# A list of operations searched anew: 44 fewer idle products and two sums of squares on TensorE

## The chip, the cores and the metric

One core of a Trainium2 chip runs the kernel. The time is that of the whole program on the device, in microseconds (us); of several runs the median is given. The engines are TensorE (PE, with PEld for its weight loads), VectorE (DVE), ScalarE (ACT), GpSimd (POOL) and SyncE (SP), which here only issues DMAs.

## What is computed

Linear attention over 4 batches, 8 heads, 576 positions of 64 numbers, then two feed-forward layers on the 2304 tokens of width 512:

```python
q_s = softmax(q, over the 64 numbers);  k_s = softmax(k, over the 576 positions)
kv  = einsum('bhsd,bhse->bhde', k_s, v);  x = einsum('bhsd,bhde->bhse', q_s, kv)   # -> (2304, 512)
xn  = x / sqrt(mean(x * x) + 1e-6) * rms_g
x   = (silu(xn @ w_gate) * (xn @ w_val)) @ w_out        # layer A, 1536 wide
out = softplus(x @ w_in) @ w2_out                       # layer B, 2048 wide
```

The weights arrive as 64-bit floats and are turned into 32-bit ones on the chip. Every large product is done as three products of rounded halves (`mm3`: high by high, high by low, low by high), on PE lines L838, L839 and L840.

## The kernel before

The tokens are cut into 6 blocks of 384 (3 chunks of 128), two blocks to a pair. Everything is unrolled, and the order of all instructions on all engines is one written list, `ORDER`, of some 3500 short tokens. Each token calls one function of the table `ops` and issues that function's instructions; the order of the tokens is the order in each engine's queue, and the semaphores between engines follow from the data. There is no loop and no priority beside it: an engine whose next instruction waits, waits. A last letter V, A or P picks VectorE, ScalarE or GpSimd for the step. `HOMES` says, for each kind of buffer, which of its places is taken in turn, so it changes whenever the list does.

The stages, as the list names them:

- Queries: `LQ` load, `Q0` maximum over the 64 numbers (L708), `QS` shift (L712), `QE` exponent, `QR`/`QI` sum and inverse (L721, L725), `QM` product (L732), `T`/`TC` transpose on PE (L740) and copy.
- Keys, per batch: `LK`/`LX` load, `K0` maxima over positions on DVE (L634, L636), `K1` transpose on PE (L644), `KM` maximum on DVE (L650), `K2` spread on PE (L657), `KS` subtract on DVE (L665), `KE` exponent on ACT, `K3` product with v on PE (L684), `K4` division on DVE (L692 to L695).
- Attention's output, per block j: `X0` product on PE (L770), `SQ` squares on ACT (L775), `XG` scaling, `XS` adds the four squares' tiles into one (L788, three steps a block), `X1` sums it over the partitions by a product with a column of ones on PE (L795, three products a block), `XD`/`XP` mean and inverse root, `X2` spread on PE (L811), `X3` scaling on DVE (L815), `HH`/`HL` the rounded halves (L835).
- Layer A: for the first four of the 12 slices of 128 plain products (`G`, `V`, `O`, with `S`, `A`, `AH`, `AL`); the other eight by seven products in place of eight (`M`, `C`, `D`, `SI`, `U`, `BH`, `BL`, `OP`, `OM`, `OC`).
- Layer B, by seven products too: `H`, `HC`, `HD`, `SP` (softplus), `BH`, `BL`, then `Y` into the output's tile, `YE` copy (L1203), `YO` store (L1214, L1211).
- Weights: `F` load, `CA` absolute value (L450, ACT or DVE), `CL` clamp (L455), `CD` shift and merge of the two words on DVE (L461, L465, L469), `CC`/`CS` halves (L483, L487), `ST`/`TU` out and back, `PS` sums for the seven products, `WH`/`WL` halves (L546, L552). Layer B's halves are stored with `KO` (L557, buffer `kept`) and loaded back with `WB` (L1164) for each of three pairs of blocks.
- `B.i.n` issues n products of the identity with itself (L885) that nobody reads: idle products. The list of before has twelve such tokens with 114 products, all in the first 65 us.

A matmul of 32-bit numbers that is not done in halves (`B`, `K1`, `K2`, `T`, `X1`, `X2`) shows as two rows of the trace.

At the end of the list, the two last `Y` complete the output's tile (pair 0, block 0, chunk 2); each tile has one copy of 512 columns and one or two stores.

Of the kernel before, what the change touches and what calls it, by code (L numbers as in the profile page):

```python
# [8 lines left out]
F32 = mybir.dt.float32  # L9
# [19 lines left out]
QM.0.1.0.P KS.0.0 CL.10.V B.5.6 LW.0 T.1 B.2.14 F.0 CD.10.0 K0.0.2.2.3.V QM.0.1.1.V K0.0.2.2.4.V K1.0.2 B.1.2 Q0.0.2  # L29
QS.0.2.0.P KM.0.2 K2.0.2 MV Q0.1.0 CA.3.A KE.0.0 CL.3.V F.5 LV.0.0.4 KS.0.2 CA.0.A CD.10.1 CL.0.V QS.1.0.0.P T.0 CD.0.0  # L30
CA.6.A QS.1.0.1.P KE.0.2 CL.6.V CD.0.1 CD.3.0 B.4.11 CD.3.1 K3.0.0 LV.0.4.8 CD.6.0 TC.0.A CA.5.A QE.1.0.0 CD.0.2 LK.1.2.2
T.2 CD.6.1 TC.2.A CD.10.2 K4.0.0 CD.3.2 K0.1.2.2.1.V LX.1 K3.0.2 K4.0.2 TC.1.A X0.0.1 SQ.0.1 X0.0.0 X0.0.3 LK.1.0.2 LG
QE.0.2.0 CC.3.A X0.0.2 K0.1.2.2.2.V SQ.0.0 CL.5.V SQ.0.2 F.2 CD.6.2 K0.1.0.2.1.V K0.1.2.2.3.V XS.0.0.1.V CA.2.A SQ.0.3
LQ.1.1 F.1 K0.1.0.2.2.V K0.1.0.2.3.V CC.0.A K0.1.2.2.4.V B.6.9 K1.1.2 XS.0.2.3.P CL.2.V F.7 QE.1.0.1 K0.1.0.2.4.V K1.1.0
XG.0.0.A KM.1.2 XS.0.0.2.P Q0.1.1 LW.1 CC.10.A XG.0.2.A QR.1.0 LV.1.4.8 QR.0.2.0 K2.1.2 QS.1.1.1.P CC.6.A QI.1.0 QS.1.1.0.P
B.7.4 KS.1.2 LK.2.2.2 CA.1.A X1.0 QI.0.2.0 KM.1.0 LV.1.0.4 XD.0 CS.10.V B.8.13 K2.1.0 QM.1.0.0.P KE.1.2 CA.7.A QE.1.1.1
KS.1.0 QM.1.0.1.P T.3 XP.0 F.9 K0.2.0.2.4.R F.4 QE.1.1.0 QM.0.2.0.P K0.2.0.2.3.R K3.1.2 X2.0 TC.3.A KE.1.0 QR.1.1 LQ.2.0
K0.2.2.2.1.V CS.6.V XG.0.3.A T.4 K0.2.2.2.2.V CS.0.V XG.0.1.A QI.1.1 CS.3.P CL.1.V QM.1.1.1.P T.5 X3.0.0 K4.1.2 X3.0.1
HH.0.0.A X3.0.2 QM.1.1.0.P TC.4.A T.6 K3.1.0 TC.5.A HH.0.2.A K4.1.0 K0.2.2.2.3.V HH.0.1.A CA.4.A LX.2 B.9.2 X0.1.2 X0.1.1
X0.1.0 SQ.1.1 HL.0.1.V SQ.1.2 SQ.1.0 CD.1.0 CD.5.0 LK.2.0.2 CL.7.V HL.0.0.P CD.1.1 X3.0.3 T.7 X0.1.3 Q0.2.0 K0.2.0.2.1.R  # L40
# [275 lines left out]
def linear_attention_swiglu_softplus_kernel(  # L316
# [16 lines left out]
    P = 128  # L333
# [943 lines left out]
```

## Time and profile before

| | us |
|---|---|
| median of 3 runs | 914.42 (912.97 to 916.19) |
| the profiled execution | 914.94 |
| its span, first to last instruction | 913.2 |
| PE busy | 894.1 (98%) |
| DVE busy | 623.9 (68%) |
| ACT busy | 408.3 (45%) |
| POOL busy | 285.1 (31%) |

PE, DVE and the others work side by side, so their busy times overlap. A busy PE may also be busy with idle products. The profile's clock column is the clock that TensorE was granted as a share of its full 2.4 GHz; 0.50 is the lower of its two levels, 1.2 GHz.

### The profile page before, as it was taken

Reading aid. Unit: us, or ns where it says so; the run is one execution under the profiler, and the core shown is the slowest. Engines: PE = TensorE matmul, PEld = TensorE weight load, DVE = VectorE, ACT = ScalarE, POOL = GpSimd, SP = SyncE. Lnnn points to the kernel's source line nnn. Section 1 sums busy time; section 2 is a strip of 40 time slices with the busy share of each in tenths; the row PEclk is TensorE's granted clock in tenths of the full one; section 3 lists DMA queues with packets and bytes.
Section 4 is the critical chain, followed back from the end, with each engine's and each line's share of the span. In section 5 each row is a group of like instructions: output and inputs, shape, how many; then the busy total and the mean of one; then the engine's idle time right before and its main releaser. Section 6 shows DMA issues by size and latency. Waiting matters only on the chain.

```text
span 913.2 us, 13708 instructions
## 1 busy us (share of the span) xinstructions
PE 894.1 (98%) x4964; PEld 842.5 (92%) x4964; DVE 623.9 (68%) x1155; ACT 408.3 (45%) x820; POOL 285.1 (31%) x250
## 2 busy tenths in 40 slices
PE   9899999999999999999999999999899999999998
PEld 8789999999999999999999998898798898989996
DVE  6999997687889998899988977836244222232221
ACT  3568455242366546566566672345131223221212
POOL 4355522345524321231212442453212143111001
PEclk9999999999999999999999999999999999999999
DMA  9994533323756999977999888896575566475702
GB/s 259 214 223 107 155 94 105 102 72 118 291 213 258 326 334 349 333 286 261 323 332 359 299 289 302 278 328 224 199 253 161 197 195 196 150 239 164 242 12 69
DMA packets 111523, 203.54 MB, mean 223 GB/s; under 512 B 30304, under 2 KB 71264, under 8 KB 111456
## 3 DMA queue, kind: packets, MB, share of 16 engines
q1 hardware_dynamic: 111456, 202.67, 66.8%
q8 instruction: 39, 0.64, 0.3%
q14 instruction: 28, 0.23, 0.1%
HBM read 155.19 MB, written 47.45 MB: 222 GB/s over the span
## 4 chain that ended last, share of the span: by engine, by line
PE 70%; DMA 11%; DVE 10%; ACT 3%; issue 2%; SPq 2%; POOL 1%; ACTq 0%; DVEq 0%; POOLq 0%
PE ps L838 23%; PE ps L839 23%; PE ps L840 22%; DMA kept<-ws 5%; DMA k_t<-in_k_dram 2%; DMA raw<-in_moe_w_in_dram 2%; DVE bits L469 1%; DVE bits L465 1%; PE ps L684 1%; DVE km_t L634 1%; SPq L594 1%; DMA xy<-outside 1%; DMA raw<-in_moe_w_val_dram 1%; PE ps L885 1%; DMA w<-kept 1%
## 5 line engine op out<-in xcount | busy, mean ns | idle before, releaser
L838 PE MATMUL ps<-hl,w 128*128 128x384 f32 x280 | 98.2, 351 | 0.2 <-DVE xy L815 0.2
L839 PE MATMUL ps<-hl,w 128*128 128x384 f32 x280 | 93.8, 335 | 0.3 <-DVE hl L835 0.3
L840 PE MATMUL ps<-hl,w 128*128 128x384 f32 x280 | 93.8, 335 | 0.0
L1179 DVE TENSOR_TENSOR s<-ps,s 128x384 f32<-128x384 f32 x48 | 26.6, 556 | 88.0 <-PE ps L840 80.2
L838 PE MATMUL ps<-xy,w 128*128 128x384 f32 x226 | 76.3, 338 | 1.0 <-DVE s L1119 0.3
L1144 POOL TENSOR_TENSOR h<-s,h 128x384 fp32r<-128x384 f32 x29 | 30.7, 1064 | 148.1 <-DVE h L1140 81.5
L840 PE MATMUL ps<-xy,w 128*128 128x384 f32 x226 | 75.9, 336 | 0.0
L839 PE MATMUL ps<-xy,w 128*128 128x384 f32 x226 | 75.8, 335 | 0.0
L1144 POOL TENSOR_TENSOR h<-a,h 128x384 fp32r<-128x384 f32 x29 | 32.1, 1111 | 128.3 <-ACT h L1140 65.8
L840 PE MATMUL ps<-w,h 128*128 128x512 f32 x180 | 71.2, 395 | 0.0
L839 PE MATMUL ps<-w,h 128*128 128x512 f32 x180 | 70.9, 394 | 0.0
L838 PE MATMUL ps<-w,h 128*128 128x512 f32 x180 | 70.1, 390 | 0.2 <-DMA w<-kept 0.2
L838 PE MATMUL ps<-h,w 128*128 128x384 f32 x192 | 64.7, 337 | 2.7 <-ACT ps L1148 2.3
L840 PE MATMUL ps<-h,w 128*128 128x384 f32 x192 | 64.2, 334 | 0.0
L839 PE MATMUL ps<-h,w 128*128 128x384 f32 x192 | 64.2, 334 | 0.0
L839 PEld LDWEIGHTS ps<-hl,w 128*128 128x128 f32 x280 | 52.6, 188 | 2.1 <-DVE hl L835 0.5
L838 PEld LDWEIGHTS ps<-hl,w 128*128 128x128 f32 x280 | 52.6, 188 | 2.1 <-DVE xy L815 0.6
L1187 ACT ACTIVATE s<-s 128x384 f32<-128x384 f32 x48 | 24.8, 524 | 64.6 <-DVE s L1179 64.5
L840 PEld LDWEIGHTS ps<-hl,w 128*128 128x128 f32 x280 | 52.6, 188 | 0.0
L469 DVE SCALAR_TENSOR_TENSOR bits<-raw,bits 128x512 int32<-128x512 int32 x62 | 49.8, 808 | 0.9
L465 DVE SCALAR_TENSOR_TENSOR bits<-raw,bits 128x512 int32<-128x512 int32 x62 | 48.6, 787 | 0.7
L450 ACT ACTIVATE bits<-raw 128x512 f32<-128x512 f32 x49 | 32.7, 672 | 31.5 <-DMA raw<-in_moe_w_in_dram 6.5
(412 smaller groups left out, 2607.8 us busy)
## 6 DMA issues: line engine op xcount, KB each, us to landing
w<-kept SPq DMA_DIRECT2D x72, 512.0 KB, 4.7
kept<-ws SPq DMA_DIRECT2D x40, 512.0 KB, 5.7
xy<-outside SPq DMA_DIRECT2D x22, 768.0 KB, 7.5
raw<-in_moe_w_out_dram SPq DMA_DIRECT2D x26, 512.0 KB, 4.4
hl<-outside SPq DMA_DIRECT2D x24, 384.0 KB, 6.6
raw<-in_moe_w_in_dram SPq DMA_DIRECT2D x16, 512.0 KB, 5.4
outside<-hl SPq DMA_DIRECT2D x18, 384.0 KB, 5.4
qe<-outside SPq DMA_DIRECT2D x8, 768.0 KB, 7.2
```

The lines of the kernel that those rows point to most:

```text
L450: nc.scalar.activation(out=b.bitcast(F32), in_=hi, func=AF.Abs)
L465: nc.vector.scalar_tensor_tensor(out=b, in0=words[:, :, 1], scalar=-0x40000000, in1=b, op0=ALU.bitwise_and, op1=ALU.bitwise_or)
L469: nc.vector.scalar_tensor_tensor(out=b, in0=words[:, :, 0], scalar=29, in1=b, op0=ALU.logical_shift_right, op1=ALU.bitwise_or)
L594: nc.sync.dma_start(out=v_t[:, m, :R, o * D:(o + 1) * D], in_=v[b, h, :SM].rearrange("(p r) d -> p r d", r=R))
L634: nc.vector.tensor_tensor(out=km, in0=km if r > 1 else k_t[:, hs, 0], in1=k_t[:, hs, r], op=ALU.max)
L684: nc.tensor.matmul(out=ps[:, i, :], lhsT=ke_t[lo][:, i, r], rhs=v_t[:, m, r, :], start=(r == 0), stop=(r == R))
L838: nc.tensor.matmul(out=ps, lhsT=wh, rhs=xh, start=first, stop=False, skip_group_check=more)
L839: nc.tensor.matmul(out=ps, lhsT=wh, rhs=xl, start=False, stop=False, skip_group_check=more)
L840: nc.tensor.matmul(out=ps, lhsT=wl, rhs=xh, start=False, stop=last, skip_group_check=more)
L1144: engine[e].tensor_tensor(out=h[:, 1], in0=part.pop((u, (f, o))), in1=h[:, 0].bitcast(F32), op=ALU.subtract)
L1179: nc.vector.tensor_tensor(out=t, in0=bk[u, "h", SEVEN[k][3]], in1=t, op=ALU.add)
L1187: nc.scalar.activation(out=t, in_=src, func=AF.Softplus)
```

## The change

`ORDER` is another list (3509 tokens for 3517), and with it `HOMES`. The kinds and numbers of the steps are the same but for these:

- `B`: six tokens with 70 products (31, 11, 13, 10, 3, 2) in place of twelve with 114.
- `XS`: 12 steps in place of 18, as blocks 0 and 1 have none; their `X1.0.4` and `X1.1.4` sum all four tiles of squares on PE, 12 products in place of 3.
- `Y.23.0.0.2` and `Y.23.0.1.2`, the last products of output tile (pair 0, block 0, chunk 2), are each split in two of 256 columns, as are this tile's copy (`YE`, one half on DVE and one on ACT) and its store (`YO`). The list's last product and store are now those of the whole tile (pair 0, block 1, chunk 2).
- Over 400 steps are on another engine than before.

The start and the end of the two lists:

```diff
-LQ.0.0 Q0.0.0 LQ.0.1 QS.0.0.0.P QS.0.0.1.V Q0.0.1 LK.0.1.1 QE.0.0.1 LX.0 MK QE.0.0.0 K0.0.1.1.1.V B.3.7 K0.0.1.1.2.V
-QS.0.1.0.V MX QR.0.0 LK.0.0.1 K0.0.1.1.3.V K0.0.1.1.4.V LK.0.2.2 QS.0.1.1.P K0.0.0.1.1.R QI.0.0 QM.0.0.1.P LQ.0.2 B.0.42
-QE.0.1.1 F.10 K1.0.0 QE.0.1.0 K0.0.2.2.1.V F.6 F.3 QM.0.0.0.P KM.0.0 K2.0.0 QR.0.1 QI.0.1 K0.0.2.2.2.V LQ.1.0 CA.10.A
...
-Y.23.1.0.2 YE.0.1.1.A YE.0.0.1.V Y.23.0.0.2 Y.23.0.1.2 YO.0.1.1 YO.0.0.1 YE.0.1.2.A YO.0.1.2 YE.0.0.2.A YO.0.0.2
+LQ.0.0 Q0.0.0 LQ.0.1 QS.0.0.1.V MK LK.0.1.1 QS.0.0.0.P QE.0.0.1 LK.0.2.2 MX Q0.0.1 K0.0.1.1.1.V LQ.0.2 QS.0.1.1.V QE.0.0.0
+QR.0.0 LX.0 K0.0.1.1.2.V QS.0.1.0.P QI.0.0 QE.0.1.1 QM.0.0.1.P K0.0.2.2.1.V QE.0.1.0 LK.0.0.1 F.5 QM.0.0.0.P CA.5.A QR.0.1
+B.0.31 T.0 QI.0.1 QM.0.1.1.P QM.0.1.0.P K0.0.1.1.3.V K0.0.0.1.1.R Q0.0.2 K0.0.2.2.2.V K0.0.2.2.3.V T.1 F.0 K0.0.2.2.4.V
+CA.0.A QS.0.2.0.V F.3 CL.5.V LQ.1.0 MV LW.0 QE.0.2.0 CA.3.A K0.0.1.1.4.V TC.1.A B.1.11 K1.0.2 K1.0.0 CL.0.V KM.0.2 F.10
...
+Y.22.1.0.1 Y.22.1.0.2 Y.23.0.1.2.0 Y.23.0.1.2.1 Y.23.1.1.1 Y.23.1.0.1 YO.0.0.1 Y.23.1.1.2 YE.0.1.0.A YE.0.1.1.A YE.0.0.2.0.V
+YE.0.0.2.1.A YO.0.1.0 YO.0.0.2.0 YO.0.0.2.1 YO.0.1.1 Y.23.1.0.2 YE.0.1.2.A YO.0.1.2
```

The functions:

```diff
     def k1m(b, lo, n):
-        nc.vector.tensor_reduce(out=t, in_=ps[:, :n * P].rearrange("p (m s) -> p m s", s=P), op=ALU.max, axis=AX.X)
+        nc.vector.tensor_reduce(
+            out=t, in_=ps[:, :n * P].rearrange("p (m s) -> p m s", s=P), op=ALU.max, axis=AX.X, negate=True
+        )
     def k2s(b, lo, n):
...
-                op=ALU.subtract,
+                op=ALU.add,
     def q0(u):
-        nc.vector.tensor_reduce(out=qs[u], in_=t, op=ALU.max, axis=AX.X)
+        nc.vector.tensor_reduce(out=qs[u], in_=t, op=ALU.max, axis=AX.X, negate=True)
     def q0s(u, r, eng):
-        eng.tensor_tensor(out=t[:, :, r], in0=t[:, :, r], in1=qs[u][:, :, r].to_broadcast([P, H, D]), op=ALU.subtract)
+        eng.tensor_tensor(out=t[:, :, r], in0=t[:, :, r], in1=qs[u][:, :, r].to_broadcast([P, H, D]), op=ALU.add)
-    def x1(j):
+    def x1(j, n=1):
         ps = rs[j] = bank()
         for c in range(NCB):
-            nc.tensor.matmul(out=ps[:, c:c + 1], lhsT=sq_t[:, 0, c * P:(c + 1) * P], rhs=ones, start=True, stop=True)
+            for m in range(n):
+                nc.tensor.matmul(
+                    out=ps[:, c:c + 1], lhsT=sq_t[:, m, c * P:(c + 1) * P], rhs=ones, start=m == 0, stop=m == n - 1
+                )
+        def side(half):
+            return slice(0, 512) if half is None else slice(256 * half, 256 * half + 256)
-        def y_mul(u, o, f, t):
+        def y_mul(u, o, f, t, half=None):
...
-            mm3(acc[jp, o, t], h[:, 0, c], h[:, 1, c], w[:, 0], w[:, 1], first, p == NPB - 1 and f != o)
+            n = side(half)
+            more = half is not None
+            last = p == NPB - 1 or (p == NPB - 2 and (i, o, t) == (2, 0, NCB - 1))
+            mm3(acc[jp, o, t][:, n], h[:, 0, c], h[:, 1, c], w[:, 0, n], w[:, 1, n], first, last and f != o, more)
```

`YE` and `YO` take a half in the same way. Four more functions are added to `ops` (`KI`, `KN` and `KX`, which subtract the keys' maxima on PE, and `QB`, which shifts, exponentiates and sums q on ACT), but no token of the list calls them.

## Rows read from the trace of the kernel before

**Rows 1.** The page, part 1: an engine's busy time (share of the span), instructions.

```profile
PE 894.1 (98%) x4964; PEld 842.5 (92%) x4964; DVE 623.9 (68%) x1155; ACT 408.3 (45%) x820; POOL 285.1 (31%) x250
```

**Rows 2.** Busy us (instructions) of each engine by stage, granted clock, DMA share, GB/s.

```profile
20.00:40.00 20.00, 15.95 (x119) 13.76 (x118) 19.61 (x41) 11.67 (x22) 5.84 (x7) 1.00 1.12 276
40.00:60.00 20.00, 19.34 (x144) 18.45 (x144) 19.39 (x42) 11.79 (x22) 12.60 (x12) 0.92 0.83 208
200.00:240.00 40.00, 40.00 (x233) 40.00 (x232) 32.70 (x51) 12.36 (x26) 22.22 (x19) 1.00 0.44 155
300.00:400.00 100.00, 98.75 (x566) 97.58 (x565) 91.45 (x179) 60.52 (x135) 26.25 (x22) 1.00 0.93 333
400.00:500.00 100.00, 98.04 (x562) 96.98 (x561) 91.44 (x177) 58.32 (x130) 23.26 (x21) 1.00 0.87 312
600.00:700.00 100.00, 96.58 (x473) 86.16 (x472) 40.85 (x71) 36.28 (x67) 29.84 (x24) 0.98 0.67 226
900.00:914.00 14.00, 9.22 (x41) 7.31 (x39) 0.69 (x1) 2.94 (x5) 0.00 (x0) 0.99 0.36 112
```

**Rows 3.** PE's timeline of the head: start us, us, instructions, [idle before].

```profile
1.34 13.31 PE L885 MATMUL ps<-ident 128*128 128x128 f32 x98 [1.34 <-POOL ident masks.py:199]
...
14.48 0.38 PE L644 MATMUL ps<-ident,km_t 128*128 128x128 f32 x2
...
42.96 0.90 PE L795 MATMUL ps<-ones,sq_t 128*128 128x1 f32 x6
...
43.72 3.15 PE L885 MATMUL ps<-ident 128*128 128x128 f32 x26
...
58.10 0.47 PE L838 MATMUL ps<-hl,w 128*128 128x384 f32 x1
```

**Rows 4.** Waits of DVE in the first 60 us: us in total, times, longest.

```profile
DVE mx L650 <- PE ps L644: 2.1, 1, 2.1
```

**Rows 5.** DVE by line and shape, 0 to 58 us: busy us, mean ns.

```profile
L634 DVE TENSOR_TENSOR km_t<-km_t,k_t 128x256 f32<-128x256 f32 x11 | 5.3, 488 | 0.1
...
L712 DVE TENSOR_TENSOR qh<-qh,qm 128x512 f32<-128x512 f32 x2 | 1.4, 688 | 0.0
...
L487 DVE TENSOR_TENSOR w<-bits,w 128x512 fp32r<-128x512 f32 x2 | 1.4, 683 | 0.0
...
L455 DVE TENSOR_SCALAR bits<-bits 128x512 f32<-128x512 f32 x3 | 1.3, 420 | 0.0
...
L788 DVE TENSOR_TENSOR sq_t<-sq_t 128x384 f32<-128x384 f32 x1 | 0.6, 553 | 0.0
```

**Rows 6.** Busy us by stretch of 2 us, granted clock behind them.

```profile
30.00:32.00 2.00, 0.42 (x4) 0.26 (x3) 1.89 (x7) 0.00 (x0) 0.00 (x0) 1.00 1.10 268
40.00:42.00 2.00, 2.00 (x10) 1.77 (x10) 2.00 (x3) 0.44 (x1) 0.60 (x1) 0.50 0.62 128
42.00:44.00 2.00, 2.00 (x14) 2.00 (x14) 1.97 (x5) 0.00 (x0) 1.54 (x3) 0.67 0.17 35
```

**Rows 7.** SP's timeline, 640 to 650 us: DMA issues.

```profile
642.04 0.42 SPq L557 DMA_DIRECT2D kept<-ws  x1
648.95 0.32 SPq L1164 DMA_DIRECT2D wf<-kept  x1
```

**Rows 8.** Busy us by stretch of 5 us, granted clock behind them.

```profile
655.00:660.00 5.00, 5.00 (x21) 4.42 (x20) 0.96 (x2) 0.32 (x1) 1.01 (x1) 0.73 0.24 70
660.00:665.00 5.00, 5.00 (x27) 4.56 (x26) 0.56 (x1) 1.65 (x4) 0.00 (x0) 1.00 0.38 141
```

**Rows 9.** Waits of PE from 160 to 860 us: us in total, times, longest.

```profile
PE ps L838 <- DMA wf<-kept: 2.3, 1, 2.3
...
PE ps L838 <- ACT a L1187: 1.1, 1, 1.1
```

**Rows 10.** Timelines of PE and ACT at the end: start us, us.

```profile
908.83 0.39 PE L840 MATMUL ps<-w,h 128*128 128x512 f32 x1
...
909.30 0.58 ACT L1203 COPY ws<-ps 128x512 f32<-128x512 f32 x1 [0.77 <-PE ps L840]
```

More of the change, by code (lines that the diff above doesn't have):

```diff
@@ L306 @@
[L306 to L311 removed]
+hl 012345012345103425340125432105210543210543214305210543052143052143210543
@@ L632, in k0 @@
         km = km_t[:, hs]
-        if how == "V":
-            nc.vector.tensor_tensor(out=km, in0=km if r > 1 else k_t[:, hs, 0], in1=k_t[:, hs, r], op=ALU.max)
+        if how in engine:
+            engine[how].tensor_tensor(out=km, in0=km if r > 1 else k_t[:, hs, 0], in1=k_t[:, hs, r], op=ALU.max)
         elif r == 1:
@@ L668, in k2s, with k_same, k_less, k_exp @@
                 in1=bc.to_broadcast([P, 2, R + 1, D]),
-                op=ALU.subtract,
+                op=ALU.add,
             )
+    kd = {}
+    def k_same(b, lo, n):
+        kd[b, lo] = [bank() for _ in range(n + 1)]
+        for i in range(n):
+            ks = k_t[:, 2 * (lo + i):2 * (lo + i + 1)].rearrange("p h r d -> p r h d")
+            nc.tensor.matmul(
+                out=kd[b, lo][i].rearrange("p (r h d) -> p r h d", r=R, d=D), lhsT=ident, rhs=ks[:, :R],
+                start=True, stop=False, skip_group_check=True,
+            )
+            nc.tensor.matmul(
+                out=kd[b, lo][n][:, i * P:(i + 1) * P].rearrange("p (h d) -> p h d", d=D), lhsT=ident, rhs=ks[:, R],
+                start=i == 0, stop=False, skip_group_check=True,
+            )
+    def k_less(b, lo, n):
+        t = mx.pop((b, lo))
+        for i in range(n):
+            most = t[:, i:i + 1].to_broadcast([P, P])
+            nc.tensor.matmul(
+                out=kd[b, lo][i].rearrange("p (r c) -> p r c", r=R), lhsT=most,
+                rhs=ident.rearrange("p (o c) -> p o c", o=1).to_broadcast([P, R, P]),
+                start=False, stop=True, skip_group_check=True,
+            )
+            nc.tensor.matmul(
+                out=kd[b, lo][n][:, i * P:(i + 1) * P], lhsT=most, rhs=ident, start=False, stop=True, skip_group_check=True
+            )
+    def k_exp(b, lo, n):
+        ps = kd.pop((b, lo))
+        for i in range(n):
+            nc.scalar.activation(
+                out=ke_t[lo][:, i, :R], in_=ps[i].rearrange("p (r c) -> p r c", r=R), func=AF.Exp
+            )
+        nc.scalar.activation(
+            out=ke_t[lo][:, :, R], in_=ps[n][:, :n * P].rearrange("p (m c) -> p m c", m=n), func=AF.Exp
+        )
     def ke(b, lo, n):
@@ L716, in q1, with q1s @@
         nc.scalar.activation(out=t, in_=t, func=AF.Exp)
+    def q1s(u, r):
+        t = q_t[u]
+        s = qs[u, r, "sum"] = take(sm_p, "qs1_", [P, H, 1, 1])
+        for h in range(H):
+            nc.scalar.activation(
+                out=t[:, h, r], in_=t[:, h, r], func=AF.Exp, bias=qs[u][:, h, r], accum_out=s[:, h, 0]
+            )
     def q2(u, r=None):
```

565 lines of the change are left out of this document (286 added, 279 removed).

## The prediction

> **What bounds the kernel now.** I read the page's busy times first, then the busy times by stage, then TensorE's timeline of the first 70 us and the lists of waits. TensorE (PE) is busy for 894.1 of 913.2 us [rows 1]. So what a new order of the same products can win is what PE does not spend on needed products: its idle time, about 19 us, and the idle products (operation `B`), of which the list of before has 114. The stages [rows 2] show where the idle time lies: 4.1 us between 20 and 40 us, 1.3 and 2.0 us in the two hundreds from 300 to 500, 3.4 us from 600 to 700, and 4.8 us in the last 14, the end of the program. In the head a second engine is as full as PE: VectorE (DVE) is busy for 19.6 of the 20 us from 20 to 40 and for 19.4 of those from 40 to 60. There the head moves forward only as fast as DVE works through its list, and the idle products fill what PE has over. From 300 to 500 DVE is at 91 of 100 us, still under PE.
>
> **The head: PE's list.** The new list has B.0.31, 11, 13, 10, 3 and 2: 70 idle products, 44 fewer. One of them (two rows each) takes 3.15 / 13 = 0.242 us in the run of 26 rows that starts at 43.72 us [rows 3], so 44 x 0.242 = -10.6 us. For two blocks (`X1.0.4`, `X1.1.4`) the sum of squares now takes 12 products of one column in place of 3, so 18 more; three of them (six rows) take 43.72 - 42.96 = 0.76 us before the next instruction [rows 3], 0.25 each: +4.6 us. The last tile's halves are 12 products of 256 columns for 6 of 512: the same columns, so between 0 and six more products' 0.185 us each (27 in 5 us [rows 8]), 1.1 in all; I take 0.1, nearest to equal columns. PE's list is 5.9 us shorter. All other products are the same in number and size; the new helpers for k (`KI`, `KN`, `KX`) and `QB` are defined but do not occur in the list.
>
> **The head: DVE's list.** An idle product that goes is only worth something if DVE comes earlier too. I count DVE's instructions up to the last `K4` of batch 1, after which the first real layer product follows: 3 fewer clamps (`CL`, 0.420 each), 3 fewer differences (`CS`, 0.683), 2 fewer maxima (`K0`, 0.488), 1 fewer sum of squares (`XS`, 0.553; the six removed `XS` were five on POOL, one on DVE), and 1 more q shift (`QS`, 0.688) [rows 5]: -1.3 - 2.0 - 1.0 - 0.6 + 0.7 = -4.2 us. Then there is a wait of the old list that its idle products made: the run of 98 rows ends at 14.65 us, and only then does PE transpose the column maxima (14.48) [rows 3], which DVE waits for, 2.1 us long [rows 4]. In the new list 31 and 11 idle products, 42 for 49, and two small transposes stand ahead of the same step; so the wait lies between all kept (0) and all gone (-2.1). I take -1.6, as 7 fewer products are 1.7 us. DVE comes 5.8 us earlier (bounds 4.2 to 6.3) at that point. PE's own list up to there is 38 x 0.242 - 9 x 0.25 = 6.9 us shorter, so DVE decides. After it, the other 6 idle products go (-1.5), and `X1.1.4` costs +2.3 and the halves +0.1 with PE full: the head is worth -5.8 - 1.5 + 2.3 + 0.1 = -4.9 us (bounds -3.3 to -5.4). The DMAs of these steps move with it: up to the first layer product SP has some 3 MB fewer to issue in the new list, and all of batch 1's v loads now stand ahead of the next batch's k load. So I cost them at nothing; if a v load is late all the same, its wait comes out of the 4.9.
>
> **The middle.** From 300 to 500 and from 600 to 700 PE idles for 6.6 us in sum [rows 2]; the new list has its own waits, which need not be these. One can be followed. The longest, 2.3 us [rows 9], is a product of layer B waiting for a converted weight which SP stored at 642.04 and could load back only at 648.95, when the store had landed [rows 7]. In the old list 27 matmuls stand between that store (`KO.66.1`) and the first product of it (`Y.7`); in the new one 45. At 0.185 us each [rows 8] this is 3.3 us more room than before, against 2.3 missing. Behind the wait PE's granted clock falls to 0.73 between 655 and 660, and PE starts 21 matmuls there instead of 27 [rows 8]: 1.1 us more. So up to -3.4. Against it stands one more pair of Abs and Softplus on ACT in that layer (five instead of four), which needs table loads; of the four pairs now one shows a PE wait, 1.1 us [rows 9]; so 0 to +1.1. The other waits of these stages (4.3 us) come anew in an unknown number: all gone, -4.3, or twice as many, +4.3. I take -2.0 for the middle, the followed wait less a good part for new ones (bounds -7.7 to +5.4).
>
> **The end.** PE's last product starts at 908.83, ACT's copy ends 1.05 us after it and the span 3.3 us later [rows 10]. The halved tile (pair 0, block 0, chunk 2) does not stand last in the new list: block 1's whole tile does, again with one copy of 512 columns and one DMA behind it. So nothing: 0, bounds -0.5 (its last stores meet less traffic) to +0.5 (two more issues on SP ahead of it).
>
> **The sum.** -4.9 - 2.0 + 0 = -6.9 us against the profiled execution, 914.94 us (span 913.2 and 1.7 around it), gives 908.0. The median of the runs is 914.42, 0.5 lower: 907.5.
>
> **A rule that speaks against it.** PE's granted clock goes down after idling: from 30 to 32 us PE is busy for 0.4 of 2 us, and from 40 to 44 the clock is 0.50 and 0.67, its lower level of 1.2 GHz for most of it [rows 6]. The Trainium skill (TensorE: Matmul & The Clock Gate, "What's actually happening") says that the throttled clock is the default and only activity releases it; by that rule fewer idle products mean a slower clock in the head, and the trace agrees in direction. By it the sum would be the second rival's, by DVE's rows it is the one above.
>
> **Rivals.** First, more comes: the head reaches its bound (-5.4) and all waits of the middle go (-7.7): -13, 901. For it: DVE's list is the shorter one in the head. Against it: any new list has some waits. Second, the clock takes it back: after the first 31 idle products, some 8 us, PE's next work is a transpose that needs the whole chain of the first q (maximum, exponent, sum, product on POOL) and may leave PE idle; the next products may then run at 1.2 GHz. A fall like that of 40 to 44 us costs 0.50 x 2 + 0.33 x 2 = 1.7 us; two of them, with a head at its lower bound (-3.3) and a middle with as many waits as now (0), leave about 0: 914. For it speaks that the old list's longest run stood just there; against it, that DVE and not PE decides in the head. Third, it gets slower, by DVE. Work moved from POOL and ACT to DVE (7 `WL`, 8 `CA`, 8 `C`, 7 `BH`, 5 `HL` among others) makes DVE's whole list about 15 us longer, summed with the means of the view that rows 5 come from. At the point where 240 us of needed products are done, DVE's list is 3.3 us longer than in the old list and PE's 6.1 shorter: DVE has 9.4 us less room when it enters the stretch where it is 91% busy. It decides if this is more than DVE idles before it, 7.3 us from 200 to 240 alone [rows 2]. Then PE gets 9.4 us of waits, and the 3.2 us that it idles from 300 to 500 double: 9.4 + 3.2 - 6.9 = +5.7, 920. Against it: between 500 and 700, where half of the moved work lies, DVE has much room.
>
> **How the numbers follow.** Forecast 0.60, more 0.12, taken back 0.17, slower 0.11. The forecast's own range is 904 to 911.5. The range 901 to 915.5 leaves out most of the slower case and the far end of the first rival. A measurement of this kernel tells about 0.3%, 2.7 us, from nothing. Faster: forecast and first rival, 0.72; same: second rival, 0.17; slower: third, 0.11.
>
> **What would show it.** Right: the first product of L838 starts about 6 us earlier than at 58.1 us [rows 3]; idle products fill some 17 us; PE shows no wait for `kept` of 2 us after the last store; PE's busy time falls by about 6 us. Wrong: a clock under 0.9 over more than 5 us of the head; PE waits for DVE between 200 and 560 us of more than 6 us; new waits of PE for transfers in layer B of over 3 us in sum.

## The result, and the profile after

The changed kernel takes 902.60 us (median of 4 executions, 901.75 to 908.07), the kernel before 915.31 on the same chip: 12.7 us less by the medians, and a ratio of 0.9875 (95% interval 0.9829 to 0.9922), which is 11.4 us. Taken again on another chip it is 903.42 against 916.57 us, ratio 0.9852 (0.9829 to 0.9876). The forecast was 907.5, with 904 to 911.5 as the forecast's own range and 901 to 915.5 as the whole one. So the direction and the whole range hold, the narrow one does not, and more came than the forecast's 6.9 us. The profiled execution happens to be the slowest of its four, 908.07 us, which is the predicted difference to the tenth (914.94 - 6.9); that agreement is luck, as the experiments show.

The page's busy times of the changed kernel, for [rows 1]:

```profile
PE 888.3 (98%) x4918; PEld 840.2 (93%) x4918; DVE 630.3 (70%) x1181; ACT 409.4 (45%) x813; POOL 263.7 (29%) x230
```

PE's busy time is 5.8 us less, as counted (5.9). The stages, for [rows 2]:

```profile
20.00:40.00 20.00, 18.91 (x140) 16.68 (x140) 18.17 (x43) 11.34 (x20) 7.79 (x8) 0.96 1.00 223
40.00:60.00 20.00, 19.93 (x140) 19.24 (x140) 19.40 (x40) 15.49 (x29) 8.37 (x8) 0.93 0.99 268
300.00:400.00 100.00, 100.00 (x577) 99.71 (x576) 93.46 (x184) 55.38 (x123) 26.22 (x25) 1.00 0.90 325
400.00:500.00 100.00, 99.63 (x574) 99.26 (x574) 93.45 (x179) 57.31 (x127) 26.19 (x23) 1.00 0.85 304
500.00:600.00 100.00, 97.15 (x493) 88.84 (x493) 76.43 (x131) 60.84 (x108) 31.45 (x27) 0.98 0.82 287
600.00:700.00 100.00, 97.71 (x480) 87.88 (x479) 49.64 (x88) 27.13 (x57) 26.66 (x19) 0.98 0.73 239
```

From 300 to 500 PE idles for 0.4 us where it idled for 3.2, and that with DVE at 93 of 100 us where it was at 91. PE's idle time is now between 500 and 700: 2.9 and 2.3 us, with a granted clock of 0.98. PE's three longest waits say what for; the first of them lies in the head:

```profile
PE ps L790 <- POOL qn L782: 3.0, 1, 3.0
PE ps L892 <- DMA w<-kept: 2.3, 1, 2.3
PE ps L892 <- ACT a L1233: 2.0, 1, 2.0
```

PE's timeline of the head, for [rows 3] (L939 is the idle product, L847 is X1, L892 the first layer product, old L885, L795 and L838):

```profile
1.34 8.59 PE L939 MATMUL ps<-ident 128*128 128x128 f32 x62 [1.34 <-POOL ident masks.py:199]
...
34.71 3.00 PE L847 MATMUL ps<-ones,sq_t 128*128 128x1 f32 x24
...
50.56 0.47 PE L892 MATMUL ps<-hl,w 128*128 128x384 f32 x1
...
55.43 2.73 PE L847 MATMUL ps<-ones,sq_t 128*128 128x1 f32 x24
```

The first layer product starts 7.5 us earlier (58.10 to 50.56). Counting layer products in both traces, the changed kernel is 8.2 us ahead at the start of the 50th (67.9 against 76.1 us) and 6.7 at the 1100th (279.6 against 286.3); by then all other kinds of products are done in both lists, so this is what the head gave. It is 9.6 ahead at the 2300th and back to 6.1 at the 2900th, behind the first wait of layer B.

How far DVE is when it ends the last `K4` of batch 1 (L695, new L736), the busy times up to there, and what it waited for PE; first before, then the changed kernel:

```profile
55.42 0.59 DVE L695 TENSOR_TENSOR kvb<-ps,den 64x128 f32<-64x128 f32 x2
0.00:56.01 56.01, 49.75 (x378) 46.76 (x378) 47.86 (x100) 26.56 (x45) 24.31 (x31) 0.97 0.94 242
DVE xy L665 <- PE ps L657: 0.3, 1, 0.3
L455 DVE TENSOR_SCALAR x<-x 128x512 f32<-128x512 f32 x4 | 2.7, 666 | 0.0
```

```profile
48.27 0.59 DVE L736 TENSOR_TENSOR kvb<-ps,den 64x128 f32<-64x128 f32 x2
0.00:48.86 48.86, 42.62 (x319) 39.52 (x320) 41.43 (x92) 24.94 (x41) 25.96 (x31) 0.97 0.98 240
DVE xy L667 <- PE ps L659: 1.6, 2, 0.9
```

DVE gets there 7.2 us earlier: it works 6.4 us less (47.86 to 41.43) and idles 0.7 less. The wait of 2.1 us for the column maxima [rows 4] is gone, but the one for K2's product (L665, new L667) has grown by 1.3. The line of L455 shows four clamps of the old list, 0.666 us each, of which the new list has one up to there.

The clock in the head, in stretches of 2 us as in [rows 6]:

```profile
38.00:40.00 2.00, 1.82 (x11) 1.55 (x10) 1.22 (x4) 0.45 (x1) 1.71 (x3) 0.61 0.85 184
40.00:42.00 2.00, 2.00 (x12) 2.00 (x12) 1.84 (x3) 0.43 (x2) 2.00 (x3) 0.54 0.96 250
58.00:60.00 2.00, 2.00 (x12) 1.87 (x12) 1.95 (x5) 1.16 (x3) 0.00 (x0) 0.73 0.88 239
60.00:62.00 2.00, 2.00 (x9) 2.00 (x8) 0.93 (x3) 1.40 (x3) 1.51 (x2) 0.50 1.10 267
```

Two falls to the lower level (1.2 GHz), each about 1.7 us of lost speed. From 48 to 58 us PE was busy without a gap, so the second does not follow idle time. Both stand a microsecond or so behind a stretch of X1.

### The profile page after: what moved, and what is told of

Its sections match the earlier page's. It is cut to its first block, busy times and chain, and to the rows that moved or that the text cites. A ratio compares the mean times of both kernels' runs of the same rounds, so it can differ in the third digit from the quotient of the medians.

```text
span 906.3 us, 13616 instructions
## 1 busy us (share of the span) xinstructions
PE 888.3 (98%) x4918; PEld 840.2 (93%) x4918; DVE 630.3 (70%) x1181; ACT 409.4 (45%) x813; POOL 263.7 (29%) x230
## 4 chain that ended last, share of the span: by engine, by line
PE 84%; DVE 8%; DMA 4%; ACT 2%; issue 1%; SPq 0%; ACTq 0%; DVEq 0%
PE ps L892 26%; PE ps L894 26%; PE ps L893 26%; DMA kept<-ws 2%; PE ps L820 2%; PE ps L725 2%; PE ps L847 1%; DMA w<-kept 1%; DMA raw<-in_moe_w_out_dram 1%; PE ps L790 1%; DVE xy L667 1%; DMA qh<-in_q_dram 0%; PE ps L659 0%; PE ps L939 0%; DVE qm L749 0%
## 5 line engine op out<-in xcount | busy, mean ns | idle before, releaser
L892 PE MATMUL ps<-hl,w 128*128 128x384 f32 x278 | 96.9, 349 | 0.0
L1202 POOL TENSOR_TENSOR h<-a,h 128x384 fp32r<-128x384 f32 x36 | 40.5, 1127 | 176.0 <-ACT h L1198 94.3
L892 PE MATMUL ps<-xy,w 128*128 128x384 f32 x246 | 83.4, 339 | 4.3 <-DMA w<-kept 2.3
L894 PE MATMUL ps<-xy,w 128*128 128x384 f32 x246 | 83.1, 338 | 0.0
L893 PE MATMUL ps<-xy,w 128*128 128x384 f32 x246 | 83.1, 338 | 0.0
L894 PE MATMUL ps<-w,h 128*128 128x512 f32 (+1 forms) x169 | 66.8, 395 | 0.0
L893 PE MATMUL ps<-w,h 128*128 128x512 f32 (+1 forms) x169 | 66.6, 394 | 0.0
L892 PE MATMUL ps<-h,w 128*128 128x384 f32 x192 | 64.8, 337 | 1.6 <-ACT ps L1206 1.3
L892 PE MATMUL ps<-w,h 128*128 128x512 f32 (+1 forms) x169 | 66.0, 390 | 0.0
L1202 POOL TENSOR_TENSOR h<-s,h 128x384 fp32r<-128x384 f32 x25 | 26.9, 1080 | 96.4 <-DVE h L1198 45.5
L892 PEld LDWEIGHTS ps<-xy,w 128*128 128x128 f32 x246 | 46.6, 189 | 7.4 <-DVE ws L546 2.7
L892 PEld LDWEIGHTS ps<-hl,w 128*128 128x128 f32 x278 | 52.4, 189 | 1.1 <-issue 0.2
```

What stands on the lines that cost most here:

```text
L892: nc.tensor.matmul(out=ps, lhsT=wh, rhs=xh, start=first, stop=False, skip_group_check=more)
L893: nc.tensor.matmul(out=ps, lhsT=wh, rhs=xl, start=False, stop=False, skip_group_check=more)
L894: nc.tensor.matmul(out=ps, lhsT=wl, rhs=xh, start=False, stop=last, skip_group_check=more)
L1202: engine[e].tensor_tensor(out=h[:, 1], in0=part.pop((u, (f, o))), in1=h[:, 0].bitcast(F32), op=ALU.subtract)
```

## Experiments

Each was timed in five rounds beside the kernel before; "the changed kernel" is e1's 903.42 us, ratio 0.9852. The experiments ran on three chips, so where two of them are compared, the ratios to the kernel before are safer than the times. Where an edit writes the list or a function anew, the line numbers move by up to 19 (L905 is L892).

### e1: the changed kernel again

> The changed kernel once more, unaltered. The timed runs of it were 901.75 to 903.34 us, its profiled execution 908.07. Theory A (what one execution loses to late transfers and to the clock behind them differs from execution to execution): the timed runs lie again at 901 to 904, and a new profile shows other waits of PE than the 2.3 us for a kept weight and the 2.0 us for ACT at L1233, or the same with other sizes, and another time. Theory B (profiling itself costs the new list 6 us, or the waits belong to the list): the profiled execution is again at 907 to 909 with the same two waits.

Measured: 901.98 to 905.12 us. The profiled execution is the slowest again (905.12); it has the same two waits of layer B, with 2.1 us for L1233's copy and 1.5 us for the kept weight, and a granted clock of 1.00 from 500 to 700 us where it was 0.98. So the places belong to the list, and how long the wait is, and whether the clock falls behind it, to the execution. Over the five executions the mean granted clock goes from 0.995 (905.1 us) to 1.00 (902.0 us); two falls of 1.7 us would make it 0.996, so by this mean the fastest execution had not even those of the head. The kernel before varies more: 912.3 to 920.1 us, at 0.993 to 1.00.

### e2, e3, e4: the idle products

```diff
 e2, the list before (114 -> 70)
-B.3.7  B.0.42  B.2.14  B.4.11  B.8.13
+B.3.2  B.0.31  B.2.4   B.4.3   B.8.3
 e3, the changed list (70 -> 114)
-B.0.31 B.1.11 B.2.13 B.3.10 B.4.3 B.5.2
+B.0.42 B.1.20 B.2.23 B.3.18 B.4.6 B.5.5
 e4, the changed list (70 -> 6)
+B.0.1  B.1.1  B.2.1  B.3.1  B.4.1 B.5.1
```

> The list of before with 70 idle products in place of 114 (counts alone: 42 to 31, 7 to 2, 14 to 4, 11 to 3, 13 to 3). Theory A (VectorE decides in the head; idle products cost only where VectorE waits behind them): 2 to 4 us less than before, ratio 0.995 to 0.998. Theory B (PE's own list decides): 44 x 0.242 = 10.6 us less, ratio 0.988. Theory C (idle products hold TensorE's clock up): granted clock at 0.5 to 0.7 over more of the first 60 us than before's 4 us, time equal or 1.7 us or more longer, ratio 1.000 to 1.005.

> The changed list with its idle products back at before's number, 114 (31 to 42, 11 to 20, 13 to 23, 10 to 18, 3 to 6, 2 to 5). Theory A (VectorE decides in the head): 1.5 to 4 us more than the changed kernel. Theory B (PE's list decides): 10.6 us more. Theory C (clock): the same time or less, with no stretch of the first 65 us under 0.9.

> The changed list with one idle product in each of its six places, 6 in place of 70. Theory A (VectorE decides in the head): 0 to 4 us less than the changed kernel. Theory B (PE's list decides): 64 x 0.242 = 15.5 us less. Theory C (the clock takes it back): granted clock at 0.5 to 0.7 over 5 to 20 us of the first 65, and 2 to 6 us more than the changed kernel.

Measured: e2 914.54 us against 916.57 of before, ratio 0.9972 (0.9955 to 0.9988), 2.0 us less. e3 908.53 (0.9906, 0.9877 to 0.9934), 5.1 over the changed kernel; its two executions at a clock of 1.00 took 904.9 and 905.3, about 3 over the changed kernel's one at 1.00. e4 904.90 (0.9873, 0.9851 to 0.9895), 1.5 over it, with overlapping intervals. None is near the 10.6 and 15.5 us of PE's own list. How an idle product costs time, if it does, is in DVE's waits of the first 60 us, in e3

```profile
DVE xy L667 <- PE ps L659: 3.9, 2, 3.0
```

and in e1:

```profile
DVE xy L667 <- PE ps L659: 1.6, 2, 0.9
```

PE works off idle products in front of the K2 that DVE waits for: 2.3 us more, and the first layer product starts at 53.64 us in place of 50.33. In e4 nothing of the kind is left to win: it starts at 50.18. But e4 shows something else, PE's first work after the idle products (columns: start us, us, instructions, idle before):

```profile
12.73 1.97 PE L790 MATMUL ps<-ident,qn 128*128 128x128 f32 x8 [10.59 <-POOL qn L782]
```

In e1 the same eight rows:

```profile
12.69 1.09 PE L790 MATMUL ps<-ident,qn 128*128 128x128 f32 x8 [1.31 <-POOL qn L782]
```

After 10.6 us of idling the same rows take nearly twice as long, and so do those of K2 at 19.5 us (2.07 for 1.06; in the changed kernel K2's eight rows take 2.07 us at 38.9 us, where the granted clock is 0.61 and 0.54). So PE is at its lower level there, and still the first layer product is not late: DVE sets the pace. The clock column reads 1.00 in these stretches of e4; the durations, not the column, show the level at the start of a program. The Trainium skill (TensorE: Matmul & The Clock Gate, "What's actually happening") calls the throttled clock the default that activity releases; these durations agree. In e2 the column itself shows it (20 to 30 and 40 to 50 us):

```profile
20.00:30.00 10.00, 7.37 (x42) 6.91 (x41) 9.07 (x17) 3.97 (x6) 3.71 (x5) 0.70 0.99 244
40.00:50.00 10.00, 8.34 (x41) 7.85 (x40) 9.15 (x16) 4.36 (x7) 6.57 (x7) 0.55 0.70 139
```

Theory B is refuted in all three, and theory A's mechanism is what the waits show; its ranges were missed in e3 (1.5 to 4 us more, measured 5.1) and in e4 (0 to 4 less, measured 1.5 more within overlapping intervals). Theory C's falls are there: e2's executions have a mean granted clock of 0.988 to 0.996 where before's have 0.993 to 1.00, and its profiled execution, the slowest of the twelve, starts the first layer product at 59.66 us, later than before's 58.10. By the median e2 gains all the same. In e3's profile the clock is as theory C said, but the time is not:

```profile
30.00:66.00 36.00, 35.23 (x262) 32.85 (x262) 34.23 (x76) 25.66 (x49) 15.00 (x14) 1.00 0.91 232
```

This stretch holds the same two stretches of X1 in one-column products (2.74 and 2.73 us), and no fall follows them.

### e5: the sums of squares back on VectorE and GpSimd

```diff
-SQ.0.2 ... SQ.0.1 ... X1.0.4
+SQ.0.2 XS.0.2.3.P ... SQ.0.1 XS.0.0.1.V XS.0.0.2.P ... X1.0
-SQ.1.2 ... SQ.1.1 ... X1.1.4
+SQ.1.2 XS.1.2.3.P ... SQ.1.1 XS.1.0.1.P XS.1.0.2.P ... X1.1
```

> The changed list with the two blocks' sums of squares back in six XS steps (two on VectorE or GpSimd before each X1) and three products in X1.0 and X1.1 in place of twelve. In the changed kernel's profile the two stretches of twelve take 3.0 and 2.7 us. Theory A (the prediction's term: the 18 small products cost 0.25 each where PE is full): 2 to 4 us less than the changed kernel's 903.4. Theory B (the steps on GpSimd, 1.0 us each, and VectorE's 0.55 make the chain to X2 longer, and the first layer product waits): 0.5 to 3 us more. Theory C (the granted clock of 0.5 to 0.6 at 38 to 42 and 58 to 62 us is due to the stretches of one-column products before it): those two falls are gone, 1.7 us less for each, on top of A, so 5 to 7 us less.

Measured: 909.21 us, ratio 0.9915 (0.9887 to 0.9943): 5.8 more than the changed kernel, past theory B's 3 and opposite to A. PE's timeline at the two X1:

```profile
39.07 0.83 PE L861 MATMUL ps<-ones,sq_t 128*128 128x1 f32 x6 [4.40 <-POOL sq_t L852]
...
60.20 1.41 PE L861 MATMUL ps<-ones,sq_t 128*128 128x1 f32 x6 [2.20 <-POOL sq_t L852]
```

What the first one waited for stands in the timelines of DVE and GpSimd:

```profile
37.34 0.55 DVE L852 TENSOR_TENSOR sq_t<-sq_t 128x384 f32<-128x384 f32 x1
```

```profile
38.03 0.99 POOL L852 TENSOR_TENSOR sq_t<-sq_t 128x384 f32<-128x384 f32 x1 [2.57 <-DVE qs L789]
```

ScalarE's four squares were done at 35.04 us. DVE's sum had its turn in a full queue 2.3 us later, GpSimd's last one started behind it (the releaser named is the DVE instruction after it) and took until 39.02. For block 1 the two sums after the last square take 2.64 us on GpSimd alone. At the 1100th layer product e5 is 5.2 us behind e1, so nearly all of the loss lies in the head. Theory C can't be told from this run: the clock falls at 40 to 44 and 60 to 68 us, but now behind the new idle times. The second fall (0.57 over these 8 us) is 3.4 us of lost speed where e1's is 1.7, so some 1.7 of the 5.2 us are the clock's. The run shows what the sums cost at the places and on the engines that e5 gives them; others were not tried.

### e6: the last tile whole

```diff
-Y.23.0.0.2.0 ... Y.23.0.0.2.1 ... Y.23.0.1.2.0 Y.23.0.1.2.1 ... YE.0.0.2.0.V YE.0.0.2.1.A ... YO.0.0.2.0 YO.0.0.2.1
+Y.23.0.0.2 ... Y.23.0.1.2 ... YE.0.0.2.V ... YO.0.0.2
```

> The changed list with output tile (pair 0, block 0, chunk 2) whole again: its products of 512 columns, one copy on VectorE, one store. Theory A (the prediction's: this tile does not end the program): within 0.5 us of the changed kernel's 903.4. Theory B (halves let the last stores start earlier): 0.5 to 1.5 us more, with a longer stretch from PE's last product to the end than the changed kernel's 5.0 us.

Measured: 903.81 us, ratio 0.9866 (0.9840 to 0.9893), 0.4 from the changed kernel. Its last product starts 4.5 us before the end of the span (896.11 of 900.6), the changed kernel's 5.1 (901.17 of 906.3), before's 4.4 [rows 10]. Theory A in time: the halves are worth nothing that can be measured. The end itself is longer with them, in all nine profiles that have halves (5.1 us) against the five without (4.3 to 4.5), the opposite of theory B. SP's timeline at the end of e1 shows why:

```profile
898.55 1.15 SPq L1278 DMA_DIRECT2D out_dram<-ws  x2
899.81 0.54 SPq L1281 DMA_DIRECT2D out_dram<-ws  x1
```

The last copy ends at 899.27 us, and its store is issued only behind two others; in e6 the copy ends at 897.16 and the store follows at 897.18.

### e7 and e10: the two waits of layer B

ScalarE's timeline in e1, before PE's wait of 2.1 us:

```profile
553.31 1.28 ACT L450 ACT_TABLE_LOAD   x1
557.87 0.66 ACT L450 ACTIVATE bits<-raw 128x512 f32<-128x512 f32 x1 [3.28 <-DMA raw<-in_moe_w_out_dram]
558.54 1.28 ACT L1245 ACT_TABLE_LOAD   x1
...
561.07 0.47 ACT L1233 COPY a<-ps 128x384 f32<-128x384 f32 x1
```

The Abs of weight 62 waits 3.3 us for its load, and the copy L1233 that PE needs is queued behind it, with a table load of 1.28 us and three other steps between the two. SP's timeline before the wait for the kept weight: a load (`we`) that waits until its own store has landed, and behind it in the queue the load (`w`) that PE needs.

```profile
615.73 0.32 SPq L1222 DMA_DIRECT2D we<-kept  x1
616.14 0.38 SPq L1222 DMA_DIRECT2D w<-kept  x1
```

```diff
 e7: both edits
-CA.62.A
+CA.62.V
-WB.7.hx3 ... WB.7.hx2
+WB.7.hx2 WB.7.hx3      (each in the place in SBUF that it had)
 e10: as e7, but
-CA.62.V ... (27 steps) ... CL.62.V
+(27 steps) ... CA.62.V CL.62.V
```

> The changed list with two edits for its two longest waits of PE in layer B: the Abs of weight 62 on VectorE in place of ScalarE (where it waits 3.3 us for its load, with the copies L1233 queued behind it), and the load of the half hx3 of pair 7 put behind that of hx2 (it holds SP up until its own store has landed). Theory A (the two waits are what they seem): 2.1 us and 1.5 to 2.3 us of PE's waits go, with 0 to 1 us of a lower clock behind each: 3.5 to 5 us less than 903.4. Theory B (the next step in line is late as well): one or both come back as a wait for another step at the same place, 0 to 1.5 us less.

> The changed list with the two loads of pair 7 in the other order, and the Abs of weight 62 on VectorE just ahead of its clamp, 28 steps later, so that neither ScalarE's nor VectorE's queue waits for this load in front of the products' copies. Theory A (the wait at 558 us is a queue behind a late load): PE's wait of 1.7 to 2.1 us for L1233's copy goes, 1.5 to 2.1 us less than the 902.5 us of the run that moved it to VectorE at its old place. Theory B (something else is late there): a wait of 1 us or more stays at this place, 902 to 903.

Measured: e7 902.54 us, ratio 0.9851 (0.9824 to 0.9877). The wait for the kept weight is gone; from 600 to 700 us PE is full:

```profile
600.00:700.00 100.00, 100.00 (x499) 89.98 (x498) 50.12 (x90) 27.61 (x56) 26.23 (x19) 1.00 0.74 246
```

The other stayed at 1.7 us, and e7's timelines of DVE and ACT say why:

```profile
556.87 1.34 DVE L459 SCALAR_TENSOR_TENSOR bits<-raw 128x512 f32<-128x512 f32 x1 [5.19 <-DMA raw<-in_moe_w_out_dram]
558.14 1.35 DVE L1215 TENSOR_TENSOR h<-a,h 128x384 fp32r<-128x384 f32 x1
```

```profile
559.57 0.48 ACT L1246 COPY a<-ps 128x384 f32<-128x384 f32 x1 [4.94 <-DVE h L1215]
```

Now DVE's queue stands behind the load, with a step that ACT needs. With the Abs 27 steps later (e10: 901.36 us, ratio 0.9837, 0.9809 to 0.9865) it is gone; 550 to 570 us in e10, and the same in e1:

```profile
550.00:570.00 20.00, 19.89 (x96) 17.16 (x96) 14.90 (x22) 7.60 (x16) 10.61 (x9) 1.00 0.92 331
```

```profile
550.00:570.00 20.00, 17.87 (x86) 15.34 (x85) 13.22 (x21) 10.11 (x18) 9.51 (x8) 1.00 0.91 338
```

So theory A for e10 by the trace, B for half of e7. In time both edits together are worth 2.1 us by the medians (1.4 by the ratios, whose intervals overlap) of the 3.6 that the two waits of e1 sum to.

### e8 and e9: two waits of the list before

```diff
 e8
-WH.66.1.A ... WB.8.hx4 ... WB.8.hx3 ... WL.66.1.V ... KO.66.1
+WH.66.1.A WL.66.1.V KO.66.1 ... WB.8.hx4 ... WB.8.hx3
 e9: as e8, and
-WH.47.4.A ... CA.52.A ... OC.7.0.3.A ... OP.8.0.0.A OC.7.0.0.A
+... OC.7.0.3.A ... OP.8.0.0.A OC.7.0.0.A WH.47.4.A CA.52.A
```

> The kernel before with one move: the low half of weight 66 (WL) and its store (KO.66.1) right behind its high half (WH), ahead of two loads that hold SP. The store then starts near 639 us in place of 642.04. Theory A (the prediction's step: the wait of 2.3 us for this store and the lower clock behind it cost 3.4 us): 2.5 to 3.5 us less than before, ratio 0.996 to 0.997, no wait of PE for kept over 1 us at 650 us and a granted clock of 1.00 there. Theory B (the loads that now come later are missed next): 0 to 1 us less, with a new wait for kept.

> The kernel before with the earlier store of weight 66 (as in the run that gave ratio 0.9965) and one more move: near 465 us ScalarE's step WH.47.4 (it waits for a store to land: 1.7 us in one execution, 4.7 in another) and CA.52 (it waits for its load) go behind the four copies OC.7.0.3, OP.8.0.0 and OC.7.0.0 that PE waits for. Theory A (before loses 1.5 us here in its profiled execution and up to 4.4 us and a slower clock in others, and the changed list has no such place): ratio 0.990 to 0.995, no PE wait for ACT over 0.5 us between 460 and 480, and the runs lie closer together than before's 912.9 to 921. Theory B (the wait only moves, since the same transfers are late): ratio 0.996 to 0.998.

Measured: e8 912.57 us against 916.53, ratio 0.9965 (0.9944 to 0.9985), 4.0 less by the medians and 3.2 by the ratio. From 640 to 660 us e8 is full at full clock:

```profile
640.00:660.00 20.00, 20.00 (x99) 17.68 (x97) 9.10 (x14) 5.28 (x10) 8.74 (x7) 1.00 0.75 250
```

where before has

```profile
640.00:660.00 20.00, 17.71 (x79) 15.22 (x78) 4.64 (x10) 2.68 (x6) 4.79 (x4) 0.91 0.58 193
```

Twenty more products at some 0.185 us, 3.7 us: the followed wait and the fall behind it were worth what the prediction said (3.4). The same profile shows how before loses more in other executions. ACT's step WH.47.4, in e8:

```profile
470.15 0.40 ACT L560 CAST ws<-ws 128x256 fp32r<-128x256 f32 x1 [4.71 <-DMA kept<-ws]
```

in the profiled execution of before:

```profile
466.91 0.41 ACT L546 CAST ws<-ws 128x256 fp32r<-128x256 f32 x1 [1.68 <-DMA kept<-ws]
```

It waits for a store to land before its buffer is free, and PE's copies queue behind it: PE waits 4.4 us there in e8, with a granted clock of 0.66 from 470 to 480, 2.2 us and 0.83 in e2, 1.5 us and 1.00 in before's own profile. e9 takes this place away: 912.50 us, ratio 0.9962 (0.9941 to 0.9982), so no less than e8 in the median, though eleven of its twelve executions lie within 910.7 to 913.9 us against e8's 909.8 to 916.8. In time this is theory B (0.996 to 0.998); of theory A the trace shows the missing wait, not the size. Its profile has other waits (1.2 us for a kept weight near 655) and, in this execution, a clock of 0.66 from 40 to 50 us.

### e11 and e12: sums of 128 equal columns, and all edits together

```diff
-nc.tensor.matmul(out=ps[:, c:c + 1], lhsT=sq_t[:, m, c * P:(c + 1) * P], rhs=ones, ...)
+nc.tensor.matmul(out=ps[:, c * P:(c + 1) * P], lhsT=sq_t[:, m, c * P:(c + 1) * P],
+                 rhs=ones[:, 0:1].to_broadcast([P, P]), ...)      # X1.0.4 and X1.1.4; XD reads each 128th column
```

> The changed kernel with the 24 products of X1.0.4 and X1.1.4 taking 128 equal columns of ones in place of one (the same sums, 128 times). An idle product of 128 columns takes 0.242 us, one of these of one column 0.25 or 0.23. Theory A (the granted clock falls behind a stretch of one-column products although PE counts as busy there): the falls to 0.5 to 0.6 at 38 to 42 and 58 to 62 us are gone, the stretches last the same, and the time is 1.7 us less for each fall, 900. Theory B (the falls come from the short idle times before, or from elsewhere): they stay, 903.4 us.

> The changed list with all three edits together: the loads of pair 7 in the other order, the Abs of weight 62 on VectorE just ahead of its clamp, and 128 columns in the products of X1.0.4 and X1.1.4. Theory A (the lower clock behind the one-column sums costs 3.4 us, and without the two waits on late transfers nothing gives it back): 901.4 less 2 to 3.4 us, 898 to 899.4 us, granted clock 1.00 from 30 to 66 us, and PE full from 600 to 700. Theory B (an earlier head meets later transfers, so the gain is given back in waits between 500 and 700 us): 901 to 902 us.

Measured: e11 902.96 us, ratio 0.9853 (0.9827 to 0.9880). Its two stretches of X1, and the time from 30 to 66 us, in which the changed kernel has its two falls:

```profile
34.72 3.10 PE L848 MATMUL ps<-ones,sq_t 128*128 128x128 f32 x24
54.92 2.84 PE L848 MATMUL ps<-ones,sq_t 128*128 128x128 f32 x24
```

```profile
30.00:66.00 36.00, 34.53 (x236) 31.15 (x235) 34.93 (x75) 27.76 (x51) 17.97 (x16) 1.00 0.97 240
```

The stretches last 0.1 us longer, and both falls are gone, as theory A said; at 200 layer products e11 is 1.9 us ahead of e1, at 1900 2.9. One profile shows this, and e12's agrees; as e3 and the fastest execution of e1 have no fall behind one-column products either, such products alone do not bring it about. The time does not follow: in this profile the two waits of layer B are at 2.3 and 2.2 us, and from 550 to 570 the clock falls to 0.91. So e12 has all three edits: 899.99 us, ratio 0.9833 (0.9809 to 0.9857); its six executions (899.1 to 901.2) lie below all five of the changed kernel's. That is 3.4 us less than the changed kernel by the medians, between the two theories' figures, but 1.7 by the ratios (before took 915.03 us beside e12), whose intervals overlap. e10, the same but for the wide sums, has 0.9837. So what the wide sums are worth in time is not shown; the trace of e12 is 1.9 us ahead of e1 at 200 layer products, as that of e11. Its stages, against those of the changed kernel above:

```profile
550.00:570.00 20.00, 19.42 (x95) 16.91 (x94) 12.46 (x19) 8.22 (x16) 9.91 (x8) 1.00 0.96 354
600.00:700.00 100.00, 99.41 (x496) 89.29 (x495) 48.93 (x87) 27.56 (x57) 26.17 (x19) 1.00 0.73 242
```

## Why the prediction was right or wrong

**PE's list, -5.9: right.** The busy time fell by 5.8 us, and 24 rows of X1 took 3.00 and 2.73 us for the 3.04 worked out.

**The head, -4.9 (bounds -3.3 to -5.4): the mechanism right, the size too small.** That PE's own list does not decide there is shown by e2 to e4; 44 idle products cost 2.0 us in the old list and 3 to 5 in the new, where the prediction had 3.1 (1.6 through DVE's wait, 1.5 where PE is full). But at the 1100th layer product the changed kernel was 6.7 (after) and 6.9 us (e1) ahead, past the bound. **The term that was mis-sized is DVE's list**: "-1.3 - 2.0 - 1.0 - 0.6 + 0.7 = -4.2 us" came out at -6.4, and the wait put at -1.6 at -0.7, since a part of it came back at K2; so DVE was 7.2 us earlier, where the prediction had 5.8 (bounds 4.2 to 6.3). A part of the difference is the price of a clamp: 0.420 each was the mean of one kind, and the three that went are of the other kind, which took 0.666 (L455 above). What was to follow, +0.9 (-1.5 + 2.3 + 0.1), came out at about +0.4. No run puts the clamps, differences and maxima back, so DVE's share is read from the traces and not from an experiment.

**A second step was wrong, X1's**: "`X1.1.4` costs +2.3", set against one DVE addition. The 2.3 is what PE spends, but the sums that it replaces were not free: with them back the changed list is 5.8 us slower (e5), since PE's path then leads through their turn in DVE's full queue and through GpSimd at 1.0 to 1.5 us a step. The five removed `XS` on GpSimd were put at nothing without a reason; the old list shows no wait for them. What they bind only shows once the rest of the head is faster. The 5.8 of e5 and the 3 to 5 of e3 are together more than the head gained: each says what the new list would lose, and they are not parts of the gain. Missed the other way were the two falls of the clock behind the one-column sums (1.7 us each by their rows; e11, without them, is 1.9 us ahead).

**The middle, -2.0 (bounds -7.7 to +5.4): the followed wait right, the rest in the bounds.** The store that stood between a weight and its product was worth -3.4 as worked out, and -4.0 as measured (e8; by its interval 1.4 to 5.1). The extra pair of Abs and Softplus was put at 0 to +1.1 for table loads; the wait there was 1.5 to 2.3 us, and not for the tables alone: a late load holds the Abs, and the copy for PE waits behind it (e7, e10). The room of 45 products did away with the wait after the last store, but another load of a kept weight came up to 2.3 us late instead. From 300 to 500 PE idles 2.8 us less. Against the profile of before the span is 9.8 us shorter in e1: 6.9 in the head, 3.7 in the middle, less 0.8 at the end; in the first profile of the changed kernel it is 6.9, with 1.0 in the middle. That the medians differ by some 13 us has a further part that no single profile shows: the profiled execution of before was 1.6 us better than its median on the second chip, the one of e1 1.7 worse than its own. e8 and e2 show one place where before's loss varies (1.5 to 4.4 us of waiting, and the clock behind it); that removing it would lower the median could not be shown (e9), so which places make up the rest stays open.

**The end, 0: right in time** (e6: 0.4, within what can be told). By the traces it is 0.6 to 0.8 us longer, just past the bound of +0.5, for the reason that went with it: more issues on SP ahead of the last store.

**The rivals.** The clock took nothing back at the place that the second one named: PE idles 3.0 us for the first q chain, and in e4 10.6, with its next rows at the lower level, and the first layer product is not late. The third, DVE as the bound from 300 to 500, is refuted: DVE is busier (93 of 100) and PE idles less; over the whole program DVE's busy time grew by 6.4 us, where this rival had its list some 15 longer. The first, "more comes, 901", is nearest in size to 902.6, and the head did go past its bound, but the middle kept waits.

**The signs named in advance.** The first layer product was to start about 6 us earlier (7.5); no wait for the kept weight after the last store (none there); PE's busy time 6 us less (5.8). Of the signs against, one came: a clock under 0.9 over more than 5 us of the head (four stretches of 2 us), and it cost up to the 3.4 us that its rows say (1.9 by e11) without turning the result. A second, waits for transfers of over 3 us in layer B, came too if the wait behind the late load of weight 62 is counted: 2.3 and 2.0 us in the first profile, 1.5 and 2.1 in e1.

## What to carry to other kernels

An idle product costs little as long as the engine that decides does not wait behind it, so look in that engine's waits and not in PE's busy time. Where another engine decides, price the steps that leave its list by what each kind of them took in that stretch. A step that hides today is not worth zero when it goes together with what hides it: ask which in-order queue it stands in, and what is ahead of it there. And a load's consumer put too early into an engine's queue makes everything behind it wait for the load; moving it to another engine moves the wait along (e7), moving it later in the list removes it (e10).

## What was not expected of the hardware

- The granted clock fell to 0.50 behind 24 rows of one-column products (2.73 us) that the trace counts as a busy PE, with no idle time for the 10 us from 48 to 58 us; with 128 columns the same rows took 2.84 us and the clock stayed at 1.00 (e11). It also stayed at 1.00 in e3, with one column and more idle products, so when the fall comes is open.
- In the first 20 us of e4 the clock column reads 1.00 while the same rows take 1.97 in place of 1.09 us.
- The same list's executions differ by 3 us (changed kernel) to 8 us (before) with the mean granted clock, 1.00 to 0.993. In the profiles the waits on late transfers vary in length (0.83 and 0.66 of granted clock behind waits of 2.2 and 4.4 us, 1.00 behind 1.5); that this makes up the whole spread is not shown.
